# Two parts of the inner width in one PSUM tile, in the first-layer chunks of 128 rows

## The chip, the cores and the metric

One core of a Trainium2 chip runs the whole program. TensorE (PE) multiplies matrices, ScalarE (ACT) evaluates functions and casts, VectorE (DVE) and GpSimd (POOL) do elementwise work, SyncE (SP) issues most of the DMAs. The metric is the device time of one execution in microseconds (us), the median of three runs. Each engine takes its instructions in a fixed order and waits on semaphores, so a wait holds up everything that stands behind it on that engine.

## The reference

Three layers follow each other. Attention with a top-32 mask, for 4 batches of 8 heads with 576 rows of width 64:

```
scores = q @ k.T / 8;  keep the scores >= the 32nd largest of their row
x = softmax(kept scores) @ v              # then put together to 2304 rows of 512
```

A gated layer of inner width 1536 (called the first layer here), and a layer of 8 experts of which every row uses two:

```
x = (sigmoid(x @ w_gate) * (x @ w_val)) @ w_out
top2 of (x @ w_gate2 + log1p(exp(x @ w_noise)) * noise);  softmax of the two
out[row] = sum over its two experts of weight * (relu(x @ w1[e]) @ w2[e])
```

## The kernel before, in words

The order of all work is written by a small list scheduler inside the kernel, the class `Plan`. Each piece of work is an `op` with an engine, an assumed duration, a priority (the smaller comes first), the ops that it waits for and the tiles that it takes and gives back. `Plan.run` plays this through with the assumed durations and writes each instruction down when its engine is free, its tiles are there and nothing of smaller priority is ready. What comes out is one fixed order for each engine. A change of durations, of the number of ops or of tiles in one place moves the order everywhere behind it.

Attention (`attention`) works on 144 score tiles of 128 rows by 576 keys, two heads at a time. For one tile: PE multiplies (L348), ACT copies the scores out (L356), DVE searches candidates (L365, L371, L374), ACT and POOL form a second key (L400, L405, L406), DVE ranks (L413) and masks (L428), PE transposes (L457, four matmuls for one tile), PE multiplies with v (L498), and DVE, ACT and POOL scale the result and split it into two halves of 16 bits (L505, L508, L511).

The first layer (`moe1`) takes 2304 rows in chunks: six chunks of 256 rows and six of 128. The small ones are the first two of batch 0, the last two of batch 3, and two that gather 64 left-over rows each of two batches (their input tile is called `xrem`, that of the others `xch`). For each chunk the inner width of 1536 is cut into 12 parts of 128. For one part PE computes the gate half and the value half into one PSUM tile `mm` (12 matmuls each, L538). Then ACT takes a tanh of the gate half (L545), DVE multiplies with the value half (L548), ACT rounds to 16 bits (L552), and POOL takes the remainder (L555). The two 16-bit halves lie in a tile `g`. The second product (L577) reads the twelve parts two at a time, in steps of 6 matmuls. There are 3 tiles `mm`, 2 tiles `th` and 10 tiles `g`. The first layer has a priority 1000 behind the attention of the same rows, so its matmuls fill what attention leaves free, while its ACT, DVE and POOL pieces have a priority 2000 ahead of that. The weights of the first layer are unpacked early in the program by DVE (L281, L282, L289), POOL (L286, L292) and ACT.

A router (L616 to L685) then picks two experts for each row, and `expert` does the last layer: gathers by POOL (L790), matmuls (L808, L834), ACT and DVE between them (L813, L816, and L735 and L738 for the weights), and scatters by POOL (L846).

Of the kernel before, what the change touches and what calls it, by code (L numbers as in the profile page):

```python
# [11 lines left out]
FT = mybir.dt.float32  # L12
# [114 lines left out]
def attention_moe_kernel(ctx: ExitStack, tc: tile.TileContext, qT, kT, v, w_gate, w_val, w_out,  # L127
# [50 lines left out]
    def layers(fast):  # L178
# [341 lines left out]
        def moe1(ch, prio):  # L520
# [4 lines left out]
            for f in range(12):  # L525
                wt = WA[f // 2]
# [3 lines left out]
                def half(a, r=r, f=f, wt=wt):  # L530
                    def fn():
                        if a == 0:
                            r.ps = tile_of("mm", [128, 2, n], FT)
                        fo = (f % 2) * 128
                        i = 0
                        for kb in range(4):
                            for c, x in ((0, 0), (0, 1), (1, 0)):
                                P.matmul(r.ps[:, a, :], wt.t[:, a, c, kb, fo:fo + 128], ch.x[x][:, kb, :],  # L538
                                         start=i == 0, stop=i == 11)
                                i += 1  # L540
                    return fn

                def th(r=r):
                    r.th = tile_of("th", [128, n], FT)
                    A.activation(r.th, r.ps[:, 0], AF.Tanh, scale=0.5 / (SX * SG))  # L545
# [4 lines left out]
                def gh(r=r):  # L550
                    r.g = tile_of("g", [128, 2, n], FH)
                    A.activation(r.g[:, 0], r.th, AF.Copy)  # L552
# [3 lines left out]
                p0 = op("PE", 12 * mmt, prio + f * 0.01, half(0), ch.ready + wt.done[0], alloc=[hm, hg], use=[ch.h, wt.h])  # L556
                p1_ = op("PE", 12 * mmt, prio + f * 0.01, half(1), [p0] + wt.done[1], use=[hm, ch.h, wt.h])
                a = op("ACT", 0.08 + n / 1400, prio - 2000, th, [p0], alloc=[ht], use=[hm])
                b = op("DVE", 0.08 + n / 1000, prio - 2000, pr, [a, p1_], use=[ht, hm])
                c = op("ACT", 0.1 + n / 1250, prio - 2000, gh, [b], use=[ht, hg])  # L560
                d = op("POOL", 0.12 + n / 460, prio - 2000, gl, [c], use=[ht, hg])
                r.h, r.done = hg, [c, d]
                gs.append(r)
            ch.x2, ch.hx2 = [], []
            evs = []
            for t in range(nt):
# [3 lines left out]
                for q in range(6):  # L570
                    def wo(r=r, t=t, q=q):
                        if q == 0:
                            r.ps = tile_of("mm", [128, DM], FT)
                        for f in range(2 * q, 2 * q + 2):
                            g = gs[f].g
                            for i, (c, d) in enumerate(((0, 0), (0, 1), (1, 0))):
                                P.matmul(r.ps, g[:, c, 128 * t:128 * t + 128], WO[f // 4].t[:, d, f % 4, :],  # L577
# [485 lines left out]
```

## Time and profile before

| | us |
|---|---|
| median of three runs | 1344.57 (1341.06 to 1346.83) |
| the profiled execution, whole | 1342.8 |
| its span, first to last instruction | 1341.0 |
| PE busy | 1193.8 |
| DVE busy | 872.2 |
| ACT busy | 800.6 |
| POOL busy | 743.0 |

The span holds three stages. Up to about 215 us the weights are unpacked beside the first attention tiles. Up to about 910 us attention and the first layer run interleaved. After that only the experts are left. Busy times of an engine are read by stage, since the share over the whole span mixes these.

### The profile page before, as it was taken

Reading aid. Unit: us, or ns where it says so; the run is one execution under the profiler, and the core shown is the slowest. Engines: PE = TensorE matmul, PEld = TensorE weight load, DVE = VectorE, ACT = ScalarE, POOL = GpSimd, SP = SyncE. Lnnn points to the kernel's source line nnn. Section 1 sums busy time; section 2 is a strip of 40 time slices with the busy share of each in tenths; the row PEclk is TensorE's granted clock in tenths of the full one; section 3 lists DMA queues with packets and bytes.
Section 4 is the critical chain, followed back from the end, with each engine's and each line's share of the span. In section 5 each row is a group of like instructions: output and inputs, shape, how many; then the busy total and the mean of one; then the engine's idle time right before and its main releaser. Section 6 shows DMA issues by size and latency. Waiting matters only on the chain. (4 is left out here: it accounts for less than half of the span.)

```text
span 1341.0 us, 29639 instructions
## 1 busy us (share of the span) xinstructions
PE 1193.8 (89%) x10669; PEld 878.2 (65%) x10670; DVE 872.2 (65%) x3616; ACT 800.6 (60%) x1796; POOL 743.0 (55%) x1004
## 2 busy tenths in 40 slices
PE   2456478699999999999999999989999999999997
PEld 1235356487676777786786876877666666676674
DVE  5998998888788688788888778545114234243111
ACT  4767778787777777786787776755214334243221
POOL 2789998788476776666775566342322222322221
PEclk9668689799899999999999999999999999999999
DMA  8433332344002500003300001357636576576441
GB/s 179 141 95 117 125 111 71 97 114 171 17 2 72 158 1 10 10 9 92 106 2 1 19 9 33 111 153 218 109 67 177 98 182 168 111 194 129 73 74 22
DMA packets 105616, 122.30 MB, mean 91 GB/s; under 512 B 56689, under 2 KB 66033, under 8 KB 105458
## 3 DMA queue, kind: packets, MB, share of 16 engines
q1 hardware_dynamic: 95346, 100.33, 27.5%
q0 software_dynamic: 10112, 19.97, 8.0%
q8 instruction: 86, 1.41, 0.4%
q14 instruction: 72, 0.59, 0.2%
HBM read 79.58 MB, written 20.63 MB: 75 GB/s over the span
## 5 line engine op out<-in xcount | busy, mean ns | idle before, releaser
L538 PEld LDWEIGHTS <-w 128*128 128x128 f16 x3456 | 275.3, 100 | 49.4 <-issue 21.7
L538 PE MATMUL mm<-xch,w 128*128 128x256 f16 (+1 forms) x2880 | 284.1, 254 | 17.8 <-DVE th L548 8.2
L816 DVE SCALAR_TENSOR_TENSOR g<-mm,g 128x256 f16<-128x256 f32 (+1 forms) x192 | 71.9, 379 | 242.5 <-ACT g L813 235.0
L406 POOL TENSOR_TENSOR y<-sS,sg 128x576 f32<-128x576 f32 x144 | 194.3, 1349 | 9.1
L808 PE MATMUL mm<-xch,w 128*128 128x256 f16 (+1 forms) x2016 | 190.3, 255 | 0.0
L808 PEld LDWEIGHTS <-w 128*128 128x128 f16 x2016 | 170.3, 98 | 23.4
L365 DVE MAX8 cand<-sS 128x8 f32<-128x72 f32 x1152 | 166.7, 217 | 21.6 <-ACT sS L356 21.2
L834 PEld LDWEIGHTS <-g 128*128 128x128 f16 x960 | 92.7, 98 | 105.6 <-DVE g L816 2.8
L577 PE MATMUL mm<-w,g 128*128 128x512 f16 x648 | 156.5, 385 | 4.1 <-POOL w L292 2.2
L428 DVE SCALAR_TENSOR_TENSOR e<-sS,good,e 128x576 f32<-128x576 f32 x144 | 144.7, 1026 | 2.1 <-ACT e L383 1.1
L348 PE MATMUL ps<-khl,qs 128*128 128x288 f16 x512 | 95.2, 315 | 57.0 <-ACT sS L356 39.4
L790 POOL DMA_INDIRECT v<-xd,ids x40 | 47.6, 1190 | 167.7 <-DVE ws L780 162.2
L813 ACT ACTIVATE g<-mm 128x256 f16<-128x256 f32 (+1 forms) x192 | 66.2, 347 | 118.0 <-PE mm L808 110.1
L846 POOL DMA_INDIRECT out<-e,ids x40 | 63.8, 1594 | 127.3 <-ACT e L843 58.7
L400 ACT ACTIVATE sg<-sS,m 128x576 bf16<-128x576 f32 x144 | 110.5, 769 | 35.4 <-POOL m L391 35.4
L413 DVE MAX8 good<-y 128x8 f32<-128x584 f32 x144 | 109.9, 763 | 28.6 <-POOL y L406 24.1
L555 POOL TENSOR_TENSOR g<-th,g 128x128 f16<-128x128 f32 (+1 forms) x144 | 92.5, 646 | 62.2 <-ACT g L552 59.6
L498 PE MATMUL tp<-pt,v 128*64 128x128 f32 (+3 forms) x1600 | 117.5, 285 | 5.4 <-ACT pt L464 2.6
L834 PE MATMUL tp<-w,g 128*128 128x512 f16 x504 | 115.3, 379 | 1.2 <-DVE g L816 1.2
L498 PEld LDWEIGHTS tp<-pt,v 128*64 128x64 f32 (+1 forms) x1600 | 85.0, 143 | 41.0 <-issue 23.9
L457 PE MATMUL tp<-ident,e 128*128 128x128 f32 x576 | 89.5, 292 | 24.6 <-DVE e L428 23.5
L577 PEld LDWEIGHTS <-g 128*128 128x128 f16 x648 | 63.0, 99 | 69.6 <-issue 8.5
(162 smaller groups left out, 2069.4 us busy)
## 6 DMA issues: line engine op xcount, KB each, us to landing
st<-w SPq DMA_DIRECT2D x64, 512.0 KB
khl<-st SPq DMA_DIRECT2D x48, 144.0 KB
st<-w_gate SPq DMA_DIRECT2D x12, 512.0 KB
st<-w_val SPq DMA_DIRECT2D x12, 512.0 KB
st<-w_out SPq DMA_DIRECT2D x12, 512.0 KB
st<-k_t SPq DMA_DIRECT2D x20, 288.0 KB
st<-q_t SPq DMA_DIRECT2D x20, 288.0 KB
out<-x SPq DMA_DIRECT2D x6, 768.0 KB
```

What stands on the lines that cost most here:

```text
L348: P.matmul(o, kqr.qs[:, t, u.q0:u.q0 + 128], kqr.khl[:, c, t, ks], start=c == 0, stop=c == 1)
L365: V.max(T[t].cand[:, 8 * c:8 * c + 8], T[t].s[:, 72 * c:72 * c + 72])
L400: A.activation(T[t].sg, T[t].s, AF.Sign, scale=-CUT[0], bias=T[t].m[:, 25:26], accum_out=T[t].m[:, 26:27])
L406: G.tensor_tensor(T[t].y[:, :S], T[t].s, T[t].sg, op=OP.mult)
L413: V.max(good[:, TILES - 1 - u.i - t:TILES + 7 - u.i - t], T[t].y)
L428: return lambda: V.scalar_tensor_tensor(T[t].e, T[t].s, good[:, TILES + 6 - u.i - t:TILES + 7 - u.i - t], T[t].e, op0=OP.is_ge, op1=OP.mul ...
L498: P.matmul(u.po[64 * s:64 * s + 64, :], VB[u.b, kb][1][:k, (2 * u.hp + s) * D:(2 * u.hp + s + 1) * D], rhs, start=kb == 0, stop=kb == NK - 1)
L538: P.matmul(r.ps[:, a, :], wt.t[:, a, c, kb, fo:fo + 128], ch.x[x][:, kb, :], start=i == 0, stop=i == 11)
L555: G.tensor_tensor(r.g[:, 1], r.th, r.g[:, 0], op=OP.subtract)
L577: P.matmul(r.ps, g[:, c, 128 * t:128 * t + 128], WO[f // 4].t[:, d, f % 4, :], start=f == 0 and i == 0, stop=f == 11 and i == 2)
L808: P.matmul(r.ps, W[kb].w[c][:, 0, f * 128:f * 128 + 128], q.x[:, 4 * x + kb, :], start=i == 0, stop=i == 11)
L834: P.matmul(r.ps, gs[f].g[:, c, 128 * t:128 * t + 128], W[4 + f // 2].w[d][:, f % 2, :], start=f == 0 and i == 0, stop=f == 7 and i == 2)
```

## The change

In a chunk of 128 rows (`n` = 128) two parts now share one PSUM tile: `fw` is 2 and `w` is 256. In a chunk of 256 rows `fw` is 1 and nothing changes. The matmuls keep their shape and number; each `op` of PE now holds 24 of them (two parts' gate halves, then two parts' value halves). The tanh, the product, the rounding and the remainder run once over 256 columns where they ran twice over 128, so a small chunk has 6 of each in place of 12, and takes 6 tiles `g` in place of 12. The second product reads its part by a column offset `c0`.

```
--- before.py
+++ after.py
@@ -522,45 +522,51 @@
             nt = n // 128
             gs = []
             mmt = n / 2400.0 + 0.004
-            for f in range(12):
-                wt = WA[f // 2]
+
+            fw = 256 // n
+            w = fw * n
+            for f0 in range(0, 12, fw):
+                wt = WA[f0 // 2]
                 hm, ht, hg = plan.tile("mm"), plan.tile("th"), plan.tile("g")
                 r = Unit()
 
-                def half(a, r=r, f=f, wt=wt):
+                def half(a, r=r, f0=f0, wt=wt):
                     def fn():
                         if a == 0:
-                            r.ps = tile_of("mm", [128, 2, n], FT)
-                        fo = (f % 2) * 128
-                        i = 0
-                        for kb in range(4):
-                            for c, x in ((0, 0), (0, 1), (1, 0)):
-                                P.matmul(r.ps[:, a, :], wt.t[:, a, c, kb, fo:fo + 128], ch.x[x][:, kb, :],
-                                         start=i == 0, stop=i == 11)
-                                i += 1
+                            r.ps = tile_of("mm", [128, 2, w], FT)
+                        for j in range(fw):
+                            fo = ((f0 + j) % 2) * 128
+                            i = 0
+                            for kb in range(4):
+                                for c, x in ((0, 0), (0, 1), (1, 0)):
+                                    P.matmul(r.ps[:, a, j * n:j * n + n], wt.t[:, a, c, kb, fo:fo + 128], ch.x[x][:, kb, :],
+                                             start=i == 0, stop=i == 11)
+                                    i += 1
                     return fn
 
                 def th(r=r):
-                    r.th = tile_of("th", [128, n], FT)
+                    r.th = tile_of("th", [128, w], FT)
                     A.activation(r.th, r.ps[:, 0], AF.Tanh, scale=0.5 / (SX * SG))
 
                 def pr(r=r):
                     V.scalar_tensor_tensor(r.th, r.th, 1.0, r.ps[:, 1], op0=OP.add, op1=OP.mult)
 
                 def gh(r=r):
-                    r.g = tile_of("g", [128, 2, n], FH)
+                    r.g = tile_of("g", [128, 2, w], FH)
                     A.activation(r.g[:, 0], r.th, AF.Copy)
 
                 def gl(r=r):
                     G.tensor_tensor(r.g[:, 1], r.th, r.g[:, 0], op=OP.subtract)
-                p0 = op("PE", 12 * mmt, prio + f * 0.01, half(0), ch.ready + wt.done[0], alloc=[hm, hg], use=[ch.h, wt.h])
-                p1_ = op("PE", 12 * mmt, prio + f * 0.01, half(1), [p0] + wt.done[1], use=[hm, ch.h, wt.h])
-                a = op("ACT", 0.08 + n / 1400, prio - 2000, th, [p0], alloc=[ht], use=[hm])
-                b = op("DVE", 0.08 + n / 1000, prio - 2000, pr, [a, p1_], use=[ht, hm])
-                c = op("ACT", 0.1 + n / 1250, prio - 2000, gh, [b], use=[ht, hg])
-                d = op("POOL", 0.12 + n / 460, prio - 2000, gl, [c], use=[ht, hg])
-                r.h, r.done = hg, [c, d]
-                gs.append(r)
+                p0 = op("PE", 12 * fw * mmt, prio + f0 * 0.01, half(0), ch.ready + wt.done[0], alloc=[hm, hg], use=[ch.h, wt.h])
+                p1_ = op("PE", 12 * fw * mmt, prio + f0 * 0.01, half(1), [p0] + wt.done[1], use=[hm, ch.h, wt.h])
+                a = op("ACT", 0.08 + w / 1400, prio - 2000, th, [p0], alloc=[ht], use=[hm])
+                b = op("DVE", 0.08 + w / 1000, prio - 2000, pr, [a, p1_], use=[ht, hm])
+                c = op("ACT", 0.1 + w / 1250, prio - 2000, gh, [b], use=[ht, hg])
+                d = op("POOL", 0.12 + w / 460, prio - 2000, gl, [c], use=[ht, hg])
+                for j in range(fw):
+                    q = Unit()
+                    q.r, q.c0, q.h, q.done = r, j * n, hg, [c, d]
+                    gs.append(q)
             ch.x2, ch.hx2 = [], []
             evs = []
             for t in range(nt):
@@ -572,9 +578,9 @@
                         if q == 0:
                             r.ps = tile_of("mm", [128, DM], FT)
                         for f in range(2 * q, 2 * q + 2):
-                            g = gs[f].g
+                            g, c0 = gs[f].r.g, gs[f].c0 + 128 * t
                             for i, (c, d) in enumerate(((0, 0), (0, 1), (1, 0))):
-                                P.matmul(r.ps, g[:, c, 128 * t:128 * t + 128], WO[f // 4].t[:, d, f % 4, :],
+                                P.matmul(r.ps, g[:, c, c0:c0 + 128], WO[f // 4].t[:, d, f % 4, :],
                                          start=f == 0 and i == 0, stop=f == 11 and i == 2)
                     last = [op("PE", 1.3, prio + 0.2 + t * 0.1 + q * 0.01, wo,
                                last + gs[2 * q].done + gs[2 * q + 1].done + WO[q // 2].done[2 * (q % 2):2 * (q % 2) + 2],
```

The scheduler writes another order for all engines from the first small chunk on. In the rows below the changed kernel's lines are numbered by its own source: L545, L548, L552, L555, L735, L813 of before are L549, L552, L556, L559, L741, L819 there.

POOL, in the first small chunk while weights are unpacked (L286 and L292 are the unpacking, L405 and L406 attention's second key). Before:

```order
L555 TENSOR_TENSOR g<-th,g 128x128 x2
L286 TENSOR_TENSOR x_1028<-x_1028,st 128x512
L292 TENSOR_TENSOR w<-x_905,w 128x512
L441 TENSOR_SCALAR m<-m 128x2
L405 TENSOR_SCALAR y<-places,m 128x8
L406 TENSOR_TENSOR y<-sS,sg 128x576
L555 TENSOR_TENSOR g<-th,g 128x128
L286 TENSOR_TENSOR y<-y,st 128x512
L555 TENSOR_TENSOR g<-th,g 128x128
```

Changed:

```order
L559 TENSOR_TENSOR g<-th,g 128x256
L286 TENSOR_TENSOR x_1051<-x_1051,st 128x512
L292 TENSOR_TENSOR w<-x_905,w 128x512
L286 TENSOR_TENSOR y<-y,st 128x512
L511 TENSOR_TENSOR xch<-px,xch 128x128
L441 TENSOR_SCALAR m<-m 128x2
L405 TENSOR_SCALAR y<-places,m 128x8
L406 TENSOR_TENSOR y<-sS,sg 128x576
L405 TENSOR_SCALAR y<-places,m 128x8
L406 TENSOR_TENSOR y<-sS,sg 128x576
L559 TENSOR_TENSOR g<-th,g 128x256
```

The four pieces of 128 columns (two stand in one row) have become two of 256, and a piece of unpacking and a step of attention have moved between them.

DVE, ahead of the masks of score tiles 137 and 138 of 144 (the L428 that ends each piece). Before:

```order
L365 MAX cand<-sS 128x8 x8
L548 SCALAR_TENSOR_TENSOR th<-th,mm 128x256 x2
L505 SCALAR_TENSOR_TENSOR px<-tp,px 128x128
L365 MAX cand<-sS 128x8 x8
L413 MAX good<-y 128x8 x2
L548 SCALAR_TENSOR_TENSOR th<-th,mm 128x256
L428 SCALAR_TENSOR_TENSOR e,m<-sS,good,e 128x576 x2
```

Changed:

```order
L443 RECIPROCAL m<-m 128x2
L365 MAX cand<-sS 128x8 x16
L371 MAX m<-cand 128x8 x2
L374 MATCH_REPLACE cand<-m,cand 128x64 x2
L371 MAX m<-cand 128x8 x2
L374 MATCH_REPLACE cand<-m,cand 128x64 x2
L371 MAX m<-cand 128x8 x2
L365 MAX cand<-sS 128x8 x16
L505 SCALAR_TENSOR_TENSOR px<-tp,px 128x128
L413 MAX good<-y 128x8 x2
L428 SCALAR_TENSOR_TENSOR e,m<-sS,good,e 128x576 x2
```

Before, three first-layer products (L548) stand between these attention steps, in the changed order none. Counted over the order from its start, 184 first-layer products of 128 columns stand ahead of these masks before and 168 in the changed order (one of 256 columns counts as two); the whole first layer has 216. On PE, counted ahead of the transposes (L457) of score tile 72 and of score tile 132, the first-layer matmuls between the two are 576 of 128 columns, 864 of 256 and 294 of L577 before, and 336, 828 and 252 in the changed order. At tile 138 the two orders have the same number again.

ACT, in the last small chunk, where the experts' weights (L735, in the changed kernel L741) are cast between its pieces. Before:

```order
L735 ACTIVATE w<-st 128x1024 x2
L690 ACTIVATE dd<-dd 128x1
L552 ACTIVATE g<-th 128x128 x2
L735 ACTIVATE w<-st 128x1024
L545 ACTIVATE th<-mm 128x128 x2
L552 ACTIVATE g<-th 128x128 x2
L735 ACTIVATE w<-st 128x1024
L545 ACTIVATE th<-mm 128x128 x2
L735 ACTIVATE w<-st 128x1024
L552 ACTIVATE g<-th 128x128 x2
```

Changed:

```order
L741 ACTIVATE w<-st 128x1024
L556 ACTIVATE g<-th 128x256
L549 ACT_TABLE_LOAD
L549 ACTIVATE th<-mm 128x256
L741 ACTIVATE w<-st 128x1024 x2
L696 ACTIVATE dd<-dd 128x1
L556 ACTIVATE g<-th 128x256
L549 ACTIVATE th<-mm 128x256
L556 ACTIVATE g<-th 128x256
L741 ACTIVATE w<-st 128x1024 x2
```

Before, each tanh row holds two pieces of 128 columns; in the changed order one of 256 columns stands there, with up to two casts of weights between.

## Rows read from the trace of the kernel before

**Rows 1.** page, busy by engine and 40 slices of the span in tenths

```profile
PE 1193.8 (89%) x10669; PEld 878.2 (65%) x10670; DVE 872.2 (65%) x3616; ACT 800.6 (60%) x1796; POOL 743.0 (55%) x1004
...
PE   2456478699999999999999999989999999999997
...
PEclk9668689799899999999999999999999999999999
```

**Rows 2.** busy us by window: PE, PEld, DVE, ACT, POOL, granted clock, DMA, GB/s

```profile
100.00:215.00 115.00, 75.80 (x735) 56.49 (x735) 105.32 (x356) 84.86 (x188) 110.40 (x122) 0.79 0.34 108
...
215.00:300.00 85.00, 71.59 (x734) 55.55 (x731) 74.83 (x367) 68.59 (x162) 68.89 (x99) 0.92 0.39 100
300.00:330.00 30.00, 30.00 (x262) 22.07 (x260) 27.21 (x109) 23.55 (x54) 26.42 (x36) 1.00 0.58 202
350.00:400.00 50.00, 44.30 (x367) 34.85 (x366) 42.08 (x233) 36.91 (x84) 31.19 (x50) 0.90 0.04 12
...
550.00:780.00 230.00, 225.92 (x2248) 174.35 (x2248) 190.92 (x991) 171.09 (x425) 151.92 (x252) 1.00 0.12 34
...
910.00:1341.00 431.00, 418.88 (x3270) 286.73 (x3268) 131.40 (x312) 140.46 (x284) 112.25 (x82) 0.99 0.56 125
```

**Rows 3.** the same windows, PE's transposes of line L457 alone (four a score tile)

```profile
215.00:300.00 85.00, 10.94 (x72) 8.08 (x72) 0.92 0.39 100
...
550.00:780.00 230.00, 25.04 (x172) 19.29 (x173) 1.00 0.12 34
```

**Rows 4.** groups by line and shape, whole span: xcount, busy us, mean ns, idle before

```profile
L555 POOL TENSOR_TENSOR g<-th,g 128x256 f16<-128x256 f32 x72 | 52.9, 734 | 27.5 <-ACT g L552 25.2 <-ACT sp L634 1.1
...
L555 POOL TENSOR_TENSOR g<-th,g 128x128 f16<-128x128 f32 x72 | 39.7, 559 | 34.7 <-ACT g L552 34.4
...
L552 ACT ACTIVATE g<-th 128x256 f16<-128x256 f32 x72 | 29.7, 413 | 15.8 <-DVE th L548 15.6
...
L548 DVE SCALAR_TENSOR_TENSOR th<-th,mm 128x256 f32<-128x256 f32 x72 | 29.5, 410 | 26.2 <-ACT th L545 20.3 <-PE tp L475 2.5 <-ACT sp L635 2.4
...
L545 ACT ACTIVATE th<-mm 128x256 f32<-128x256 f32 x72 | 27.4, 381 | 49.4 <-PE mm L538 43.8 <-POOL g L555 3.6 <-POOL m L441 1.6
...
L552 ACT ACTIVATE g<-th 128x128 f16<-128x128 f32 x72 | 21.2, 306 | 4.9 <-DVE th L548 4.6
...
L548 DVE SCALAR_TENSOR_TENSOR th<-th,mm 128x128 f32<-128x128 f32 x72 | 19.5, 279 | 26.7 <-ACT th L545 20.8 <-ACT pt L464 2.5 <-PE mm L538 2.2
...
L545 ACT ACTIVATE th<-mm 128x128 f32<-128x128 f32 x72 | 19.5, 274 | 28.1 <-PE mm L538 23.0 <-POOL g L555 3.1 <-POOL m L391 1.4
```

**Rows 5.** POOL groups of line L555 in 100 to 215, then 215 to 300

```profile
L555 POOL TENSOR_TENSOR g<-th,g 128x128 f16<-128x128 f32 x18 | 11.7, 661 | 0.0
...
L555 POOL TENSOR_TENSOR g<-th,g 128x256 f16<-128x256 f32 x5 | 3.9, 774 | 0.0
```

**Rows 6.** timeline of POOL, line L555: start us, us, engine, what

```profile
117.81 0.43 POOL L555 TENSOR_TENSOR g<-th,g 128x128 f16<-128x128 f32 x1
...
399.73 0.67 POOL L555 TENSOR_TENSOR g<-th,g 128x256 f16<-128x256 f32 x1 [0.31 <-ACT g L552]
```

**Rows 7.** timeline of PE: start us, us, what, count, idle before it and releaser

```profile
371.00 3.77 PE L538 MATMUL mm<-xch,w 128*128 128x256 f16 x24
380.71 2.78 PE L538 MATMUL mm<-xch,w 128*128 128x256 f16 x24
...
840.68 1.50 PE L538 MATMUL mm<-xch,w 128*128 128x128 f16 x24 [1.88 <-DVE th L548]
872.90 6.64 PE L577 MATMUL mm<-w,g 128*128 128x512 f16 x30
897.16 1.50 PE L538 MATMUL mm<-xch,w 128*128 128x128 f16 x24 [1.89 <-DVE th L548]
902.38 2.84 PE L538 MATMUL mm<-xch,w 128*128 128x128 f16 x48
```

## The prediction

> **What bounds the kernel now.** I read the page first: the 40 slices show PE busy in full tenths from about the ninth slice to the end, and below that before [rows 1]. So the stages have to be read apart, and the windows of busy time do that [rows 2]. The reader is to see four things there. From 100 to 215 us POOL is busy 110.4 of 115 us and VectorE 105.3, PE only 75.8: unpacking the weights beside attention is bound by POOL, with VectorE close behind. From 215 to 300 no engine is full: VectorE 88%, PE 84%, POOL 81%, ACT 81%; there attention runs at the pace of its own chain. From 550 to 780 PE is busy 225.9 of 230 us: PE sets the time. From 910 on only the experts are left, with PE busy 418.9 of 431 us. From about 300 us on, then, the end is PE's work plus PE's idle time, and the change alters no matmul. It can only move PE's idle time, by what happens before PE is full, by waits of PE inside the first layer, or by how the new order shares PE's work out.
>
> The profiled execution took 1342.8 us, span 1341.0 and 1.8 around it. The median of three is 1344.57, so 1.8 us are added at the end.
>
> **What it removes.** Six small chunks have 72 parts, which become 36 pairs. By the groups by line and shape [rows 4], two of 128 columns against one of 256 cost ACT 2 x 274 - 381 = 167 ns for the tanh and 2 x 306 - 413 = 199 ns for the rounding, VectorE 2 x 279 - 410 = 148 ns, POOL 2 x 559 - 734 = 384 ns. Over 36 pairs that is 13.2 us of ACT, 5.3 of VectorE and 13.8 of POOL. Nearly all of it lies where PE is the limit and is worth nothing there: the time is filled by PE's matmuls. Two places are left.
>
> *First place, 100 to 215 us.* Eighteen of the 24 parts of the first two small chunks run there, at 661 ns each on POOL [rows 5]. The nearest row of 256 columns, in the window behind, is 774 ns, so a pair saves at most 2 x 661 - 774 = 548 ns, and nine pairs 4.9 us. Without other traffic the two shapes took 0.43 and 0.67 us [rows 6], which makes 0.19 a pair and 1.7 us. Below, nothing excludes a gain of zero, since unpacking has moved between these pieces in the order. VectorE saves 9 x 148 ns = 1.3 us in the stretch and stands 5.1 us below POOL [rows 2]; it takes over as bound only when nearly all of POOL's 4.9 are gained. I take 2.5 us, nearer to the undisturbed rows, with 0 and 4.9 as ends. What is gained there is kept: attention starts its later tiles so much earlier, and PE idles less before it is full.
>
> The long times in the stretch are shown by its mean of 661 ns beside 0.43 for the same instruction alone. The Trainium skill, "SBUF — State Buffer", section "SBUF: two separate sides", says that VectorE and GpSimd share one pair of ports by an exclusive lock held for a whole instruction. By that rule the excess is waiting and not work, the merged instruction also holds the port longer at a time, and only the 1.7 us of the undisturbed rows would be sure. The sum below would be 0.8 us later by it, and 2.4 us earlier if the whole mean were POOL's own.
>
> *Second place, waits of PE in the last chunks.* PE waits for VectorE's product in line L538 for 1.88 us at 840.7 and 1.89 us at 897.2 [rows 7], and all three tiles `mm` are full then. Before, three tiles hold 3 x 24 matmuls, by the row of 48 in 2.84 us [rows 7] 4.3 us of PE's work. Afterwards they hold 3 x 48, 8.5 us, so ACT and VectorE may be late by 4.3 us more before PE notices. Both stalls should go: 3.8 us. The new order puts up to two casts of weights between the pieces on ACT there, so a new one can come; ends 0 and 3.8, and I take 3. What is late next is the remainder of the last pair, which ends later by the longer pieces: (381 - 274) + (410 - 279) + (413 - 306) + (734 - 559) = 0.52 us [rows 4]. It is hidden by the thirty matmuls of the second product that need only earlier parts, 6.6 us [rows 7].
>
> **What it adds or moves.** An `op` of PE now holds 24 matmuls of 128 columns, 2.84 / 2 = 1.4 us, so attention's matmuls can wait that long behind one. A chunk of 256 rows has long had ops of 12 matmuls in half of 2.78 us [rows 7], the same length. I cost it at nothing; attention's queue of finished score tiles hides it. The value half of a tile now starts 12 matmuls later and frees the tile later; the doubled depth of the tiles covers that. Six tiles `g` in place of twelve of ten let the second small chunk's matmuls go ahead of the first one's second product. That falls where PE has a third of its time free, and is worth nothing by itself.
>
> *The new order.* This is the term that can cost. Counted in the order, between the transposes of score tiles 72 and 132 PE has 240 fewer matmuls of 128 columns, 36 fewer of 256 and 42 fewer of the second product. By rows that is 240 x 2.84 / 48 = 14.2, 36 x 2.78 / 24 = 4.2 and 42 x 6.64 / 30 = 9.3, together 27.7 us [rows 7]. They are done between tiles 132 and 138, where PE is then full. That costs nothing if PE stays full in between too, and PE's lack of work there if not. From 550 to 780 there are 172 transposes [rows 3], 43 tiles: a tile takes 230 / 43 = 5.35 us, with 225.9 / 43 = 5.25 of PE and 190.9 / 43 = 4.44 of VectorE [rows 2]. Without 27.7 / 60 = 0.46 us PE needs 4.79 a tile. VectorE needs 4.39, since 16 fewer products of 279 ns fall on 60 tiles, under 0.1 us a tile. At 91% of VectorE, as from 300 to 330, where 27.2 of 30 us were busy beside a full PE [rows 2], a tile takes 4.39 / 0.907 = 4.84 us and PE idles 0.05 x 60 = 3 us. At 88%, as from 215 to 300, it is 4.99 and 12 us. At 84%, as from 350 to 400, it is 5.22 and 26 us. Before, PE idles 4.1 us for 43 tiles, which is 5.7 for 60, and that goes. The net is -2.7, +6.3 and +20. I take +2, between the first two and nearer to 91%, since only that row has PE full as it will nearly be here; the ends are -3 and +20.
>
> Elsewhere the order is another one too. The gap of 350 to 400 us shows what one such accident costs: PE is busy 44.3 of 50 us at a clock of 0.90 [rows 2], and 24 matmuls that take 2.78 us took 3.77 [rows 7]. That is 5.7 us of idle time and 0.1 x 50 = 5 of clock. It may go or come a second time, 11 us either way; I take 0.
>
> **Sum.** 1342.8 - 2.5 - 3 + 2 = 1339.3 for an execution like the profiled one, and with 1.8 for the median 1341.1, called 1341.
>
> **Rivals.**
>
> *A. More is gained.* Both stalls go whole (3.8), POOL gives its 4.9 us, the deferral costs nothing, and half the gap of 350 to 400 closes, 5 us: 1342.8 - 13.7 + 1.8 = 1331; without the gap it is 1336. For it: POOL is full at 96% in its stretch, so it is truly the bound there. Against it: that mean of 661 ns contains waiting for VectorE, which has little idle time to give.
>
> *B. Slower: attention cannot use the PE time that the new order leaves it.* Between tiles 72 and 132 a tile goes on taking what attention's own chain allows, VectorE is held at 84 to 85% of its time, PE idles some 20 us net, and the 27.7 us of deferred matmuls are paid afterwards in full: 1342.8 + 20 - 5.5 + 1.8 = 1359. For it: from 350 to 400 VectorE had no more than 84%, and 88% from 215 to 300, with PE not full. Against it: from 300 to 330 VectorE was at 91% beside a full PE, and POOL and ACT have room from 550 on. It decides from a pace of about 4.95 us a tile. With idle gaps PE's clock also falls: in the stretch from 350 to 400 the granted clock is 0.90, between the level of 2.4 GHz and that of 1.2. The Trainium skill, "TensorE: Matmul & The Clock Gate", section "What's actually happening", has the half clock as the default that only activity lifts; the trace agrees with its 3.77 us in place of 2.78 behind the gaps.
>
> *C. Nothing.* The pieces were hidden everywhere and the two stalls are taken over by the waits of another instruction: 1342.8 + 1.8 = 1344.6. For it: 13 us each of ACT and POOL lie beside a full PE.
>
> **How the numbers follow.** Some 0.5% (6.7 us) is what a measurement of this kernel can tell from no change, since its three runs spread by 5.8 us; faster is below 1337.9, slower above 1351.3. My forecast has 0.50, with a range of its own of 1334 to 1348, and one fifth of it lies below 1337.9. A has 0.22, nearly all faster; B has 0.18, nearly all slower; C has 0.10 and is no change. That makes 0.28 faster, 0.53 the same and 0.19 slower. The range reaches to A's near end and most of B: 1329 to 1356.
>
> **What would show it.** Lines L545, L548, L552 and L555 should each have 36 instructions fewer, the merged ones at 256 columns with the known means. POOL's stretch from 100 us should reach the end of unpacking 2 to 3 us sooner. PE should not wait for L548 in the last small chunks. Between score tiles 72 and 132 PE's idle time should be about 8 us and VectorE at about 90%; if PE idles 20 us or more there, B holds. The experts' stage should last 431 us as before. The forecast is wrong if that stage changes, if the matmuls' rows change, or if a new gap with a falling clock appears that none of these parts names.

## The result and the profile after

The changed kernel takes 1352.98 us (median of 11 executions, 1348.66 to 1354.98), the kernel before 1341.46 beside it: a ratio of 1.0077 on record (1.0086 by the two medians), 95% interval 1.0066 to 1.0088. That is slower. It is 12 us above the forecast of 1341, though inside its range, and 11.5 us above the kernel before where 3.5 us less were forecast.

The page first, then the windows, as in [rows 1] and [rows 2].

```profile
PE 1202.8 (89%) x10669; PEld 887.9 (66%) x10670; DVE 875.4 (65%) x3580; ACT 793.5 (59%) x1724; POOL 737.6 (55%) x968
```

```profile
100.00:215.00 115.00, 80.90 (x860) 66.63 (x860) 104.66 (x327) 83.94 (x177) 104.08 (x110) 0.80 0.34 108
215.00:300.00 85.00, 67.05 (x544) 50.05 (x543) 70.99 (x346) 62.08 (x137) 65.83 (x91) 0.82 0.39 99
...
350.00:400.00 50.00, 43.00 (x392) 34.88 (x391) 48.73 (x254) 39.99 (x93) 34.23 (x54) 0.93 0.04 12
550.00:780.00 230.00, 224.18 (x2274) 174.72 (x2274) 192.41 (x973) 175.16 (x417) 146.97 (x244) 1.00 0.12 34
```

VectorE, ACT and POOL have 36, 72 and 36 instructions fewer. From 100 to 215 us POOL's busy time fell by 6.3 us, as the change should do. From 215 to 300 PE lost 4.5 us of busy time and the granted clock fell from 0.92 to 0.82.

To place the loss I read from PE's timeline when it begins the last of the four transposes (L457) of certain score tiles, the experts' first matmul, and the seventh part of expert 0's third chunk ("entry done"; "the entry" is the stretch between these two). Us from the span's start; `lats` and `hold` are told below:

| | tile 18 | 30 | 36 | 54 | 72 | 132 | experts begin | entry done | end of PE |
|---|---|---|---|---|---|---|---|---|---|
| before | 179.7 | 246.4 | 280.4 | 364.3 | 455.1 | 780.4 | 907.7 | 959.3 | 1332.0 |
| after | 169.0 | 255.1 | 291.2 | 373.2 | 462.1 | 762.0 | 910.0 | 969.7 | 1343.6 |
| `hold` | 174.0 | 250.1 | 291.3 | 364.8 | 467.9 | 778.2 | 904.7 | 959.7 | 1332.3 |
| `lats` | | 250.1 | 286.4 | 368.3 | | | 903.7 | 952.4 | 1325.3 |

Tiles are only landmarks, since the orders put different other work between them. The last three columns stand at the same work in all. By the experts' first matmul the changed kernel is only 2.4 us late. The entry takes it 59.7 us in place of 51.7, which is 8.0 more; the rest of the experts adds 1.2. So most of the 11.6 us is lost within 60 us. PE idles 7.6 us there in place of 1.9, and at a half clock loses another 3.2 (sum of one minus the granted clock, while busy).

The 2.4 us ahead of the experts weigh less. Six of the traces below (after, `after_pc`, `lat7`, `split`, `split_lats` and `lats`) have the same order on PE up to the experts' first matmul, and begin it at 910.0, 909.3, 907.6, 903.9, 904.8 and 903.7 us. A single execution does not tell a few microseconds there.

The waits of PE by line in that place, from 905 to 970 us, of the kernel before:

```profile
PE mm L808 <- DVE g L816: 1.8, 1, 1.8
```

and after (columns: us in total, times, longest):

```profile
PE mm L814 <- DVE g L822: 7.0, 3, 4.9
```

The timelines after, by engine, show what stood before that product on VectorE:

```profile
947.91 2.72 PE L814 MATMUL mm<-xch,khl 128*128 128x256 f16 x12 [4.86 <-DVE g L822]
...
947.32 0.15 DVE L785 CAST ids<-tb 128x1 int32<-128x1 f32 x1 [7.46 <-DMA tb<-tab]
947.39 0.14 DVE L786 TENSOR_SCALAR ws<-tb 128x1 f32<-128x1 f32 x1
947.45 0.41 DVE L822 SCALAR_TENSOR_TENSOR g<-mm,g 128x256 f16<-128x256 f32 x1
...
942.23 0.37 ACT L819 ACTIVATE g<-mm 128x256 f16<-128x256 f32 x1
948.43 1.06 ACT L741 ACTIVATE w<-st 128x1024 f16<-128x1024 f32 x1 [5.84 <-DMA st<-w]
...
942.68 0.34 SPq L782 DMA_DIRECT2D tb<-tab  x1
943.13 6.22 SPq L725 DMA_DIRECT2D st<-w  x3
...
931.86 2.05 POOL L691 DMA_INDIRECT tab<-wk,sl  x1 [16.67 <-DVE sl L687]
937.38 3.35 POOL L691 DMA_INDIRECT tab<-wk,sl  x1 [3.12 <-DMA tab<-wk,sl]
```

Read from the bottom. POOL writes the last router's places into the table (L691); SP reads the table back (L782); VectorE converts what was read (L785) and waits 7.46 us for it. The product that PE needs (L822) stands behind that conversion and runs the moment it is done, and PE has waited 4.86 us; its next twelve matmuls take 2.72 us at a granted clock of 0.50 (1.2 GHz), where 24 took 2.78 at 1.00 [rows 7]. ACT waits 5.84 us in the same way for an expert's weights. SP stood at the table read until the write had landed, and issued their load behind it. SP's waits from 915 to 960 us have the row

```profile
SPq L782 <- DMA tab<-wk,sl: 4.7, 1, 4.7
```

The same places in the kernel before:

```profile
942.34 1.47 PE L808 MATMUL mm<-xch,khl 128*128 128x256 f16 x12 [1.78 <-DVE g L816]
...
941.75 0.15 DVE L779 CAST ids<-tb 128x1 int32<-128x1 f32 x1 [4.24 <-DMA tb<-tab]
...
940.06 0.80 SPq L776 DMA_DIRECT2D tb<-tab  x2
...
931.57 1.00 POOL L685 DMA_INDIRECT tab<-wk,sl  x1 [16.59 <-DVE sl L681]
935.74 1.02 POOL L685 DMA_INDIRECT tab<-wk,sl  x1 [1.11 <-DMA tab<-wk,sl]
```

The wait was there before and cost 1.78 us; the two writes of the table took 1.0 us each. The way over the table was shorter too: from the read's issue to the conversion 1.7 us, in the changed kernel 4.6. Why that read took longer no run shows.

### The profile page after: what moved, and what is told of

Read it like the earlier page. It is cut to its first block, busy times and chain, and to the rows that moved or that the text cites. A ratio compares the mean times of both kernels' runs of the same rounds, so it can differ in the third digit from the quotient of the medians.

```text
span 1353.1 us, 29463 instructions
## 1 busy us (share of the span) xinstructions
PE 1202.8 (89%) x10669; PEld 887.9 (66%) x10670; DVE 875.4 (65%) x3580; ACT 793.5 (59%) x1724; POOL 737.6 (55%) x968
## 5 line engine op out<-in xcount | busy, mean ns | idle before, releaser
L822 DVE SCALAR_TENSOR_TENSOR g<-mm,g 128x256 f16<-128x256 f32 (+1 forms) x192 | 71.9, 379 | 237.5 <-ACT g L819 235.1
L406 POOL TENSOR_TENSOR y<-sS,sg 128x576 f32<-128x576 f32 x144 | 194.6, 1351 | 9.1
L840 PEld LDWEIGHTS <-g 128*128 128x128 f16 x960 | 92.8, 98 | 107.3 <-DVE g L822 3.7
L583 PE MATMUL mm<-w,g 128*128 128x512 f16 x648 | 153.4, 380 | 2.1 <-POOL w L292 2.1
L428 DVE SCALAR_TENSOR_TENSOR e<-sS,good,e 128x576 f32<-128x576 f32 x144 | 143.4, 1018 | 6.8 <-ACT e L383 5.5
L819 ACT ACTIVATE g<-mm 128x256 f16<-128x256 f32 (+1 forms) x192 | 65.7, 346 | 115.0 <-PE mm L814 107.7
L559 POOL TENSOR_TENSOR g<-th,g 128x256 f16<-128x256 f32 x108 | 83.9, 777 | 70.6 <-ACT g L556 69.9
L457 PE MATMUL tp<-ident,e 128*128 128x128 f32 x576 | 92.6, 298 | 24.9 <-DVE e L428 19.9
L383 ACT ACTIVATE e<-sS,m 128x576 f32<-128x576 f32 x144 | 107.0, 766 | 0.2
```

Of the source, the lines that this page charges most:

```text
L383: A.activation(T[t].e, T[t].s, AF.Exp, bias=T[t].m[:, CM:CM + 1], scale=SC)
L406: G.tensor_tensor(T[t].y[:, :S], T[t].s, T[t].sg, op=OP.mult)
L428: return lambda: V.scalar_tensor_tensor(T[t].e, T[t].s, good[:, TILES + 6 - u.i - t:TILES + 7 - u.i - t], T[t].e, op0=OP.is_ge, op1=OP.mul ...
L583: P.matmul(r.ps, g[:, c, c0:c0 + 128], WO[f // 4].t[:, d, f % 4, :], start=f == 0 and i == 0, stop=f == 11 and i == 2)
L840: P.matmul(r.ps, gs[f].g[:, c, 128 * t:128 * t + 128], W[4 + f // 2].w[d][:, f % 2, :], start=f == 0 and i == 0, stop=f == 7 and i == 2)
```

## The experiments

All were timed beside the kernel before (1340.2 to 1341.0 us in the five comparisons); n is the number of executions, the interval is of 95%. Line numbers in quotes are those of the kernel changed.

**Instruction or order.** `split` keeps the new tiles and order, and issues each merged instruction as two of 128 columns:

```
-A.activation(r.th, r.ps[:, 0], AF.Tanh, ...)
+for j in range(fw):
+    c = slice(j * n, j * n + n)
+    A.activation(r.th[:, c], r.ps[:, 0, c], AF.Tanh, ...)
...
```

> The changed kernel with its tiles and its order kept, but each merged instruction (tanh, product, rounding, remainder) issued as two over 128 columns, as before. Theory O (the written order makes the loss): as slow as the changed kernel, 1350 to 1358 us, since the 13 us of ACT, 5 of VectorE and 14 of POOL that come back lie beside a full PE, and the wait of PE for L822 of some 5 us at the entry of the experts is still there. Theory I (the merged instruction makes the loss, by its longer chain from matmul to free tile): back to 1341 to 1345 us.

The others merge in two of the six small chunks only. `first2` has `fw = 2 if n == 128 and not ch.rem and ch.k0 < 2 else 1` (batch 0), `rem2` has `fw = 2 if ch.rem else 1` (the left-over rows), `last2` has `ch.k0 > 2` (batch 3).

> Only the first two small chunks (batch 0) are merged, the other four stay as before. Theory O: PE runs dry between 220 and 260 us as in the changed kernel (granted clock 0.55 to 0.85 there, 0.84 to 1.0 before), which is worth 3 to 6 us by score tile 54; the entry of the experts falls by chance of the order: 1341 to 1351 us. Theory I: a third of the loss, 1345 us, and no gap.

> Only the two chunks of left-over rows are merged. They run beside a full PE. Theory O: no change before their place, first tiles as before, and afterwards only what the new order does at the entry of the experts: 1338 to 1350 us, with any difference placed after 900 us. Theory I: a third of the loss, 1345 us, as a slower pace between 550 and 780 us.

> Only the last two small chunks (batch 3) are merged. Theory O: up to 830 us as before within 2 us; the two waits of PE for L548 (3.8 us) go, and the entry of the experts decides: with the casts of expert 1's weights behind as in the changed kernel it loses 5 to 9 us (1343 to 1348), without that it gains 2 to 4 (1337 to 1340). Theory I: a third of the loss, 1345 us, in the last chunks themselves, before 910 us.

| | us (n) | ratio, interval | entry us |
|---|---|---|---|
| `split` | 1348.6 (6) | 1.0065, 1.0047 to 1.0082 | 58.0 |
| `first2` | 1349.5 (6) | 1.0071, 1.0057 to 1.0085 | 53.5 |
| `rem2` | 1351.3 (6) | 1.0088, 1.0069 to 1.0106 | 54.9 |
| `last2` | 1345.5 (12) | 1.0032, 1.0019 to 1.0044 | 60.7 |

`split` has no merged instruction, only the order, and is 8 us slower than before. That is between the two expectations and nearer to theory O: the order makes most of the loss. Of the 4 us between `split` and the whole nothing can be said, since their intervals overlap. The parts alone lose 9, 11 and 5 us where the whole loses 11.5, so the losses don't add up. `rem2` has the order of before on PE until about 530 us, `last2` until about 840, and they lose 3.2 and 9.0 us at the entry all the same. `rem2` loses more ahead of it, in two waits for VectorE's product in the last small chunks, which it leaves unmerged:

```profile
889.44 5.66 PE L542 MATMUL mm<-xch,w 128*128 128x128 f16 x72 [3.95 <-DVE th L552]
...
901.79 4.47 PE L542 MATMUL mm<-xch,w 128*128 128x128 f16 x48 [4.10 <-DVE th L552]
```

So a new order can cost at another place than the entry, too.

**What VectorE waits for.** `after_pc`, `last2_pc` and `before_pc` do the table's two conversions on POOL:

```
-V.tensor_copy(q.ids, q.tb[:, :, 1])
+G.tensor_copy(q.ids, q.tb[:, :, 1])
...
-b = op("DVE", 0.15, prio - 2000, conv, [a], use=[ht])
+b = op("POOL", 0.5, prio - 2000, conv, [a], use=[ht])
```

> The changed kernel with the two small conversions of an expert's table (L785, L786) on POOL, which gathers by them, in place of VectorE. Theory Q (at the entry of the experts PE loses 5 to 8 us because VectorE stands at this conversion, waiting for the table's DMA, with PE's products queued behind it): PE's wait of 4.9 us for L822 near 943 us goes, the stretch from the experts' first matmul to the third chunk's end is 4 to 8 us shorter, 1344 to 1349 us in all. Theory C (the chain from the last router over the table to the gathered rows is the bound there): the wait moves to the third chunk's first matmul, time as the changed kernel, 1351 to 1355 us.

> Only the last two small chunks merged, and the conversions on POOL. Theory Q: its 6 us of lead at the experts' first matmul are kept in place of lost: 1334 to 1340 us, faster than the kernel before. Theory C: the lead is lost to a wait for the third chunk's rows, 1343 to 1347 us as without the move.

> The kernel before with the same move of the conversions to POOL. Theory Q: the one wait of 1.8 us there goes, so 1337 to 1341 us against 1340.6 to 1341.5 of before, and the gain is a quarter to a third of what the changed kernel gains by it. Theory C: no change or, by the moved order, either side by up to 5 us.

They took 1348.1 us (ratio 1.0052, 1.0031 to 1.0072), 1342.3 (1.0012, 0.9997 to 1.0027) and 1340.9 (1.0002, 0.9988 to 1.0015): 5, 3 and 0 us come back. `after_pc` lies in theory Q's range, `last2_pc` between its two, and in `before_pc` the 1.78 us do not come back. `after_pc` is the narrowest of all these runs: but for the two conversions every engine has the order of the changed kernel, so its 5 us are what their place on VectorE costs more than one on POOL. Its entry still takes 56.9 us, and its timelines show the second wait, ACT's for an expert's weights, which holds up VectorE's cast of the same weights (L744) and so the product behind it:

```profile
949.20 1.47 PE L814 MATMUL mm<-xch,khl 128*128 128x256 f16 x12 [3.54 <-DVE g L822]
...
947.59 1.23 DVE L744 SCALAR_TENSOR_TENSOR w<-st,w 128x1024 f16<-128x1024 f32 x1 [5.15 <-ACT w L741]
...
946.50 1.06 ACT L741 ACTIVATE w<-st 128x1024 f16<-128x1024 f32 x1 [5.39 <-DMA st<-w]
```

**The early gap.** In `hold` each merged pair takes two of the ten tiles `g`, as two parts did before, so that the second small chunk cannot run ahead:

```
+hgs = [plan.tile("g") for _ in range(fw - 1)]
-p0 = op("PE", ..., alloc=[hm, hg], ...)
+p0 = op("PE", ..., alloc=[hm, hg] + hgs, ...)
...
```

> The changed kernel, but each merged pair takes and holds two of the ten tiles g, as two parts did before, so the second small chunk's matmuls have to wait for the first one's second product again. Theory G (with half the tiles g the second small chunk runs ahead, PE then has nothing to fill attention's waits from 220 to 260 us, and its clock falls): the granted clock from 240 to 260 us is back at 0.8 or more, score tile 54 is reached within 3 us of the kernel before (8.9 us later in the changed kernel), 1344 to 1350 us in all. Theory H (the gap comes from the order of attention and the routers after the merged pieces, whatever the tiles): clock below 0.7 in that stretch and 1350 to 1356 us.

1344.7 us (12; ratio 1.0031, 1.0019 to 1.0043): 8 us come back, but not where the theory of the tiles had them. From 220 to 280 us the kernel before and the changed kernel have

```profile
220.00:280.00 60.00, 47.27 (x489) 35.46 (x485) 53.55 (x286) 47.93 (x113) 45.71 (x69) 0.89 0.37 92
...
220.00:280.00 60.00, 43.42 (x315) 30.96 (x314) 49.07 (x249) 42.30 (x89) 45.08 (x62) 0.74 0.41 103
```

(their stretches of 350 to 400 us are in [rows 2] and above), and `hold`

```profile
220.00:280.00 60.00, 40.73 (x344) 29.49 (x342) 54.81 (x252) 42.46 (x88) 42.43 (x58) 0.83 0.31 80
...
350.00:400.00 50.00, 49.99 (x464) 40.11 (x464) 43.63 (x243) 40.05 (x95) 29.21 (x51) 1.00 0.04 12
```

The run-ahead is gone (432 first-layer matmuls ahead of tile 24, against 576 after and 480 before), and the early gap is not: tile 36 is 10.9 us late, as in the changed kernel, and from 240 to 260 us the granted clock is 0.66, not 0.8. What went is the gap of 350 to 400 us that the kernel before has too [rows 2]; by it tile 54 comes within 0.5 us of the kernel before, as the theory had it for another reason. At the experts' first matmul `hold` is 5.3 us ahead of the changed kernel, no more than executions of one order differ by, and its entry takes 55.0 us in place of 59.7. The theory falls as stated: a gap went, but another one.

**Both waits.** In `after_tp`, `before_tp` and `hold_tp` POOL issues the table read as well, so that SP's weight loads are not behind it; `hold_pc` is `hold` with the conversions alone moved.

```
-nc.sync.dma_start(q.tb, tab[...])
+nc.gpsimd.dma_start(q.tb, tab[...])
...
-a = op("SP", 0.1, prio, table, rows, alloc=[ht, hx], lat=2.5)
+a = op("POOL", 0.5, prio, table, rows, alloc=[ht, hx], lat=2.5)
```

> The kernel after with the table's conversions on POOL, and the table read itself issued by POOL too instead of SP; PE's order is the same up to the experts' stage. The loss so far: from the experts' first matmul to the end of expert 0's third chunk PE takes 51.6 us before, 59.7 after, 56.9 with only the conversions moved (1348.1 us). Theory W (SP's queue): the experts' weight loads stand behind the table read in SP's queue, so ACT's weight cast at 946.50 waits 5.39 us for its load, the evictions behind it on ACT and VectorE come late and PE waits 3.54 us. With the read gone from SP that ACT wait falls under 2 us, PE's wait near 949 under 1 us, the stretch to 52 to 54 us, the time to 1342 to 1345 us. Theory C (the way from the last router over the table to the gathered rows is the limit, whoever issues it): the stretch stays 56 us or more and the time 1347 to 1350 us.

> The same move (read and conversions on POOL) in the kernel before, which waits 1.78 us at that place. Theory W: 1338 to 1341 us, at most the 1.8 us of that wait to gain. Theory C: 1340 to 1343 us, no change, or a loss if the chain grows by POOL's own queue.

> The kernel after, its merged pairs taking two of ten tiles g (1344.7 us alone), and the conversions on POOL (3 to 5 us in the two other versions that lose there). If the two add up: 1340 to 1342 us. If the gain of the tiles g was itself had at the entry of the experts and not in the early stage (the trace of it has the early deficit as after: score tile 36 begins 10.9 us late), the two don't add: 1343 to 1346 us.

> As the last, with the table read on POOL too. Theory W: its entry loses 3.4 us (55.0 us against 51.6), of which 2 to 3 come back: 1341 to 1343 us. Theory C: as hold, 1344 to 1346 us. Under both, merging by itself gains nothing, so not under 1339 us.

With the read on POOL all lose: 1357.2 us (1.0117, 1.0097 to 1.0138), 1348.5 (1.0052, 1.0033 to 1.0071) and 1348.6 (1.0055, 1.0037 to 1.0072). PE's wait near 949 is gone from `after_tp`, and so are ACT's for weights there, as the theory of SP's queue wants. But its entry takes 59.7 us as without any move, against the 52 to 54 of that theory: ACT waits 4.87 and 4.05 us for weights near 920 and 926, and PE 3.55 us for VectorE's product near 923 and 2.95 us for the router near 930. And a new wait has come just ahead of the entry, for a remainder on POOL, whose order now holds the read as well:

```profile
910.65 1.04 PE L583 MATMUL mm<-w,g 128*128 128x512 f16 x4 [3.45 <-POOL g L559]
```

All three have it (3.45 to 4.40 us near 911), so their totals say nothing of the theory, and SP's part in the loss has no test of its own. `hold_pc` took 1339.1 us (12; 0.9980, 0.9969 to 0.9992): without the entry's loss (52.4 us) the merged kernel is no slower than before.

**The plan's own numbers.** `lat7` and `lats` leave every instruction of the changed kernel on its engine, and its order on PE until the experts' stage. The other engines have the same order too until about 890 us (`lat7`) and 815 us (`lats`). The two only tell the plan of longer times: the table read at 7.0 us in place of 2.5 (`lat7`), and the experts' weight loads at 6.0 in place of 3.0 as well (`lats`).

```
-a = op("SP", 0.1, prio, table, rows, alloc=[ht, hx], lat=2.5)
+a = op("SP", 0.1, prio, table, rows, alloc=[ht, hx], lat=7.0)
...
-a = op("SP", 1.6, p, load, alloc=[hs], lat=3.0)
+a = op("SP", 1.6, p, load, alloc=[hs], lat=6.0)
```

> The kernel after with one number of the plan changed: the table read is planned to take 7.0 us instead of 2.5, so that the written order of VectorE has fewer products of the experts' first layer behind the two conversions that wait for it. No instruction changes engine, and PE's order is the same up to the experts' stage. Theory Q (VectorE stands in order before the table's conversions): VectorE's wait of 7.46 us stays but nothing that PE needs is behind it, PE's wait of 4.86 us near 943 falls under 2 us, the stretch from the experts' first matmul to the end of expert 0's third chunk falls from 59.7 to 53 to 56 us, the time from 1353 to 1346 to 1349 us, as with the conversions on POOL (1348.1). Theory C (the way over the table is the limit): 1351 to 1354 us.

> As the last, and the loads of the experts' weights planned at 6.0 us instead of 3.0, so that ACT's and VectorE's casts of late weights stand later in the order too. Theory W (what remained with the conversions on POOL, 56.9 us in the stretch, is ACT's and VectorE's wait for weights whose loads stand behind the table read in SP's queue): stretch 51 to 54 us, 1343 to 1346 us. If W is false it is as the last, 1346 to 1349, or later where weights come too late.

> The same number changed in the kernel before, which waits only 1.78 us there. Q and W: 1338 to 1342 us, as before. If instead any change of the order in this stage costs several microseconds by itself (the order of before being a lucky one): 1344 us or more.

| | us (n) | ratio, interval | entry us |
|---|---|---|---|
| after | 1353.0 (11) | 1.0077, 1.0066 to 1.0088 | 59.7 |
| `lat7` | 1342.9 (12) | 1.0018, 1.0004 to 1.0032 | 51.1 |
| `lats` | 1338.1 (11) | 0.9984, 0.9973 to 0.9995 | 48.7 |
| `before_lat7` | 1341.8 (11) | 1.0005, 0.9996 to 1.0014 | 54.2 |

So the written order of the experts' entry makes the loss: one number gives back 10 us and two give 15, more than was expected of either. Of the 19.0 us between the two profiled executions of the changed kernel and `lats`, 11.0 lie in the entry and 6.3 ahead of it, where PE's order is the same. The way over the table is not the limit in `lat7`: SP issues the read 32.3 us behind the experts' first matmul, in the changed kernel 32.6, and the entry is 8.7 us shorter all the same. SP and VectorE in `lat7`, in the same place:

```profile
939.91 0.33 SPq L782 DMA_DIRECT2D tb<-tab  x1
...
943.50 0.75 DVE L822 SCALAR_TENSOR_TENSOR g<-mm,g 128x256 f16<-128x256 f32 x2
944.16 0.14 DVE L785 CAST ids<-tb 128x1 int32<-128x1 f32 x1
```

and VectorE in `lats`, where the read is issued earlier as well, 28.0 us behind that matmul:

```profile
932.98 0.41 DVE L822 SCALAR_TENSOR_TENSOR g<-mm,g 128x256 f16<-128x256 f32 x1
933.48 0.15 DVE L785 CAST ids<-tb 128x1 int32<-128x1 f32 x1
933.55 0.14 DVE L786 TENSOR_SCALAR ws<-tb 128x1 f32<-128x1 f32 x1
933.61 0.41 DVE L822 SCALAR_TENSOR_TENSOR g<-mm,g 128x256 f16<-128x256 f32 x1
```

Products and weight casts now stand ahead of the conversion, and it no longer waits. PE is busy again from 907 to 970 us, 61.13 us before, 55.39 after and 60.88 in `lats`:

```profile
907.00:970.00 63.00, 61.13 (x484) 42.83 (x483) 24.84 (x74) 25.09 (x51) 20.23 (x17) 1.00 0.67 164
```

```profile
907.00:970.00 63.00, 55.39 (x402) 37.31 (x401) 28.87 (x71) 26.43 (x46) 20.44 (x14) 0.95 0.66 170
```

```profile
907.00:970.00 63.00, 60.88 (x492) 43.44 (x490) 27.90 (x77) 26.51 (x50) 21.38 (x17) 1.00 0.72 176
```

`before_lat7` shows that a change of the order in this stage need not lose: its time is that of before, though its entry is 2.5 us longer. What `lat7` and `lats` leave open is the share of each wait, since they write the order of every engine in this stage anew, PE's too; only `after_pc` moves one wait alone, for 5 us.

**Is merging worth anything under that plan?** Both numbers in the kernel before, in `split` and in `hold`:

> The kernel before with both planned times changed (table read 7.0, the experts' weight loads 6.0): what the pieces of 128 columns give under the plan that gave 1338.1 us with the merged ones. If merging itself gains nothing: 1336 to 1341 us. If merging was worth the 2 to 4 us that PE's two late waits and POOL's relief were forecast at, and only hidden by the experts' entry: 1340 to 1343 us, 2 to 4 us over the merged version.

> The merged version's tiles and order with two instructions in place of each merged one, and both planned times changed. Its difference to the merged version under the same plan (1338.1 us) is the instruction alone, without the order. If the instructions gain nothing: 1336 to 1341 us. If they gain by themselves: 1341 to 1344 us.

> The merged version whose pairs take two of ten tiles g (it was 5.4 us ahead at the experts' first matmul), with both planned times changed. If what was gained before the experts' stage is now kept, 1333 to 1337 us. If the way over the table takes it back at the entry, 1337 to 1341 us.

`before_lats` took 1337.5 us (8; 0.9966, 0.9949 to 0.9983), `split_lats` 1339.4 (12; 0.9993, 0.9982 to 1.0004), beside 1338.1 with merging: the same within their intervals. So no gain from merging shows under this plan, by its instructions or by its order, and the lowest of the medians has none of it. `hold_lats` took 1345.4 us (5; 1.0037, 1.0025 to 1.0050), above both of its ranges. In its trace PE is 7.2 us ahead of before at the experts' first matmul and loses 6.3 of it in the entry, 5.03 in one wait for gathered rows (`924.12 ... [5.03 <-DMA xch<-v]`). The table did not hold them up: its conversions were done by 906.4 us. POOL's second gather for them then waited for rows to be written:

```profile
916.02 0.96 POOL L799 DMA_INDIRECT v<-xd,ids  x1 [5.38 <-DMA xd<-y]
```

That execution took 1341.6; the other 4 us of the median are not explained.

## Why the prediction was wrong, point by point

- **Pieces of 128 and 256 columns: right.** The groups of [rows 4] after:

```profile
L556 ACT ACTIVATE g<-th 128x256 f16<-128x256 f32 x108 | 44.3, 411 | 19.0 <-DVE th L552 18.8
...
L549 ACT ACTIVATE th<-mm 128x256 f32<-128x256 f32 x108 | 41.0, 379 | 81.8 <-PE mm L542 76.8 <-POOL g L559 4.7
...
L552 DVE SCALAR_TENSOR_TENSOR th<-th,mm 128x256 f32<-128x256 f32 x108 | 44.3, 411 | 61.6 <-ACT th L549 48.9 <-PE mm L542 12.4
...
L559 POOL TENSOR_TENSOR g<-th,g 128x256 f16<-128x256 f32 x108 | 83.9, 777 | 70.6 <-ACT g L556 69.9
```

  108 of each, 36 fewer, ACT and VectorE at the known means. POOL's rose from 734 to 777 ns; from 100 to 215 us a merged piece took 836, where the prediction took 774 from the next window. Its row of 0.43 us "without other traffic" was not that: VectorE's product (L548) ran beside it from 117.85 us on.

- **First place, 2.5 us from POOL's relief: wrong.** POOL was relieved, by 6.3 us, and tile 18 came 10.7 us sooner. But `split` reaches tile 18 at 167.2 us, sooner still, with POOL busy for 108.6 us from 100 to 215: the lead comes with the order, without the merged pieces. By tile 30 the changed kernel was 8.7 us late. The step that failed here is "What is gained there is kept". PE ran out of work (43.4 us busy of 60, at a clock of 0.74, from 220 to 280; 47.3 of 60 at 0.89 before). I had priced the freed tiles `g` as "worth nothing by itself". `hold` shows that the run-ahead is not the whole cause of the gap either; why this order has one stays open. All traces with this early order have the gap (in `lats`, the mildest, tile 36 is 5.9 us late). It did not set the end: by the experts' first matmul 2.4 us were left, and `lats` keeps that early order and ends below the kernel before.

- **Second place, 3 us of late waits: right.** Neither wait for VectorE's product in the last small chunks came back. From tile 144 to the experts' first matmul PE took 39.0 us in place of 44.2 and idled 4.0 less: the 1.89 us of the second wait, and 2.0 of a wait for the router (`892.17 ... PE L660 ... [2.04 <-DVE both L653]`) that the prediction had not named.

- **The new order between tiles 72 and 132, +2 us; rival B: the deferral is harmless and B false.** That stretch took 299.9 us in place of 325.3, so attention did use what PE left it, and the deferred work was done by tile 138 without loss: from tile 72 to tile 144 PE took 408.9 us in place of 408.4. PE's idle time up to tile 132 was 9.1 us (7.2 before), near the 8 that I named. VectorE was not at the 90% that I named beside it: from 550 to 780 it had 192.4 us in place of 190.9, 84%. The 4.39 us a tile that I gave VectorE should have been 4.37 (4.44 less 16 x 0.279 / 60), which makes the three net figures of this term 1 to 2 us lower and changes nothing in the outcome.

- **"The experts' stage should last 431 us as before": this is the step that decided.** From their first matmul to the end PE took 433.6 us in place of 424.3: 9.3 us for which the sum has no term. The prediction names a change of that stage as a sign of being wrong, but gives it no chance and no price. I had looked for a wait behind the one removed ("what is late next") inside the first layer alone. But the plan writes the experts' order too, and with it how many products stand behind the table's conversion. The kernel before had the wait of 4.24 us on VectorE in its trace, with 1.78 of it reaching PE. A question to that trace of what is queued behind the waiting instruction would have shown the place; that the wait could grow to 7.46 us, with 4.86 of it reaching PE, only the changed kernel's trace shows.

- **The start of the sum.** The 1.8 us that it adds for the median came from three executions (1344.57). Eleven have their median at 1341.46, so the 1341 that stood for a gain of 3.5 us is the time of the kernel before.

- **Rivals.** A came only in its late waits. B had the sign and not the place. C had the right core, that the pieces were hidden, as `before_lats` against `lats` shows; its time of 1344.6 is 8 us short, since it has no loss.

## What to carry to other kernels

Where a list scheduler writes the order, a change's price is not in the instructions that it removes: ask of every in-order engine which instruction waits for a DMA, and what stands behind it that PE needs. A planned transfer time below the real one makes such an order fragile: the plan had 2.5 us for the table read, which took 4.6 us from its issue to its conversion in the changed kernel and 1.7 in the kernel before. Two larger planned times brought the changed kernel 15 us and the kernel before 3 to 5; merging 72 parts into 36 brought nothing that shows. Test a merge by issuing the merged instruction as two in the same order before crediting or blaming the instruction.

## What the hardware showed that was not expected

POOL's issue of an indirect DMA is stretched where VectorE is at a cast with two SBUF operands. The table write took 1.00 us on POOL alone, and 2.05 and 3.35 us where VectorE's weight casts ran (`936.38 3.47 DVE L744 ... x3`). In the twenty traces 30 table writes behind 890 us took 1.27 us or more, up to 3.51. Each of them began while such a cast ran and overlapped casts by 0.4 to 2.6 us. The 49 others took 0.97 to 1.12 us; three of them began in the last 0.3 us of a cast, the rest before one or with none beside them. The Trainium skill, "SBUF — State Buffer", section "SBUF: two separate sides", says that POOL cannot write the descriptors of its own DMAs while VectorE, in a mode that uses both port pairs, holds the pair that they share. These rows show the same beside an instruction of another kind, with two SBUF inputs. The same page of the Trainium skill infers that one of that kind, `tensor_tensor`, does not stall them. Whether descriptors were held up here, or POOL's reading of its operands `wk` and `sl` from SBUF, no run tells. In the changed kernel the two writes took 3.4 us more than in the kernel before (1.05 + 2.33), part of the longer way over the table.
